# Pooled attention and top-1 experts on one core: a split opening, tied gathers, a bank for early turns, one branch at the end

## The chip, the cores and the metric

The kernel runs on one core of one Trainium2 chip. The metric is the device time of one execution in microseconds, as the median of several runs; the profile is of one execution and has a time of its own.

## The reference

Attention over 8 batches, 8 heads, 1152 positions of 64 features, with the mean of each two neighbouring queries taken first (576 queries). Its output, 4608 tokens of 512 features, goes to a layer of 8 experts: each token goes to the expert with the largest gate logit, and the result is weighted by that expert's softmax value.

```python
q_pool = q.reshape(B, H, S // 2, 2, D).mean(axis=3)
scores = scale * np.matmul(q_pool, k.transpose(0, 1, 3, 2))
scores = scores - np.max(scores, axis=-1, keepdims=True)
attn = np.exp(scores)
attn = attn / (np.sum(attn, axis=-1, keepdims=True) + 1e-09)
attn_out = np.matmul(attn, v)
x = attn_out.transpose(0, 2, 1, 3).reshape(B * S // 2, H * D)
logits = x @ w_gate
expert_idx = np.argmax(logits, axis=1)
for e in range(E):
    mask = expert_idx == e
    h = np.maximum(x[mask] @ w1[e], 0.0)
    out[mask] = gate_w[mask, None] * (h @ w2[e])
```

## The kernel before, in words

The program is a list of steps, each with an engine, an estimated time, a key, the steps it follows and the buffers (`Hold`) it uses. `Flow.emit` plans all of them: an engine that is free takes the ready step with the lowest key whose buffers are free, in a simulated time that uses the estimates. The order found is written out as each engine's instruction stream; from then on every engine, and every DMA queue, goes through its own list in order and stops at a semaphore if what it needs is not there. `carry` is a step that issues DMAs, with a second step for their flight.

**Attention.** 32 pairs of heads (`attend`, four per batch). `load_pair` issues k, q and v of a pair, four DMAs each, all on SP's queue; k has two buffers (`kp`), q one (`qn`), v three (`vn`). Pieces of k and q are 32 floats, 128 bytes. VectorE (first pair) or GpSimd (all others) adds the two neighbours of q (`qp`), VectorE turns q in two halves and k in threes of its nine chunks (`turn_q`, `turn_k`). `scores` (L530) makes 9 chunks for each half of the queries; VectorE takes each out of PSUM and keeps the row's extreme (L534); ScalarE makes exponentials (L562); GpSimd adds chunks for the row sums (L622); TensorE makes the product with v (L666). `routing` follows each batch: logits with the gate's weights `wg` (L743), the best expert, the token's place in its expert's list, and a store of the tokens' rows to `x_runs` in DRAM.

**Experts.** Sixteen slots, one after the other: 3 early and 6 wide ones of 384 tokens, 7 of 256. `tokens_of` loads a piece of an expert's list and gathers the tokens' rows with indirect DMAs on GpSimd's queue (L974), 12 for a wide slot and 8 for a small one, into `xr` and `xq`. `turn_tokens` weighs the rows (L1133, VectorE) and turns them: early slots on TensorE into PSUM tiles of the kind `py` (L1147), the others on VectorE (L1136). The result is split in two halves, `xh` and `xl`, of which there is one copy. `split_weights` does the same to the weights. `first_products` (L1210) makes `ph`, out of which ScalarE and VectorE make `hh` and `hl` (L1216, L1218); `second_products` (L1237) makes `py`, ScalarE scales it to `y` (three buffers), and GpSimd scatters `y` to the output (L1244).

**End.** `slot_table` and `flag` have left three numbers in `stab`. Every engine loads one, branches over a second, exact attention (L1324, L1326), loads two more and passes a loop over further slots (L1343 to L1353). With these inputs neither is entered.

Of the kernel before, what the change touches and what calls it, by code (L numbers as in the profile page):

```python
# [30 lines left out]
K_V = -40  # L31
# [33 lines left out]
TURN = 3  # L65
FILL = 3
# [193 lines left out]
def kernel(  # L260
# [89 lines left out]
    for g in range(NB):  # L350
        nc.gpsimd.iota(iot[g * BL:(g + 1) * BL], pattern=[[1, NJ]], base=g * NJ, channel_multiplier=NB * NJ)
# [54 lines left out]
    def open_attention(exact, base, pairs, units):  # L406
# [9 lines left out]
        o.exact = exact  # L416
        o.turned, o.marks = [], []
# [42 lines left out]
    def load_pair(o, f, key, b, hp):  # L460

        x = Pools()
        kp = tile_of(o, "kp", [P, NQD, NC, BL], bufs=2, pool=o.ld)
        qn = tile_of(o, "qn", [P, NB, NJ, 2, BL], pool=o.ld)
# [6 lines left out]
        load = lambda out, src: nc.sync.dma_start(out=out, in_=src)  # L471

        def quarters(t, src):

            for h in range(2):
                for i in range(D // BL):
                    g = (h * D // BL + i) * BL
                    load(t[g:g + BL], src[h][:, i * BL:(i + 1) * BL].rearrange("(p n) d -> p n d", p=BL))

        k0 = f.carry("SP", 1900, lambda: quarters(kp.t.rearrange("p b c d -> p (b c) d"), heads(k, b, hp)), key + K_LOAD, (), [kp], 2600)  # L480
        q0 = f.carry("SP", 1900, lambda: quarters(qn.t.rearrange("p b j t d -> p (b j t) d"), heads(q, b, hp)),
                     key + K_LOAD, (), [qn], 2600)
        vb = heads(v, b, hp).rearrange("h (p b c) d -> b p h (c d)", b=NQD, c=NC)
        x.v = f.carry("SP", 1900, lambda: [load(vn.t[i * BL:(i + 1) * BL].rearrange("p h c d -> p h (c d)"), vb[i]) for i in range(NQD)],
                    key + (-30 if opening else K_V), (), [vn], 2600)
        e, eng, ns = ("DVE", nc.vector, dve) if opening else ("POOL", nc.gpsimd, pool)
        q1 = f.add(e, ns(NJ * QP), lambda: eng.tensor_tensor(
            qp.t.rearrange("p j b d -> p b j d"), qn.t[:, :, :, 0, :], qn.t[:, :, :, 1, :], ALU.add), key + K_POOL,
            done(q0), [qn, qp])
        key += K_PIECE  # L490
        x.k, x.q = {}, {}

        def turn_k(c0, n):
            nc.vector.transpose(kT.t.rearrange("p (c b i) -> p b c i", b=NQD, i=BL)[:, :, c0:c0 + n], kp.t[:, :, c0:c0 + n])

        def turn_q(half):
            js = slice(half * NJ // 2, (half + 1) * NJ // 2)
            nc.vector.transpose(qT.t.rearrange("p (j b i) -> p j b i", b=NB, i=BL)[:, js], qp.t[:, js])  # L498

        def turned(half):  # L500
            x.q[half] = done(f.add("DVE", turn_ns(HQ), lambda: turn_q(half), key + 7 * half, done(q1), [qT, qp]))
# [3 lines left out]
        for c0 in range(0, NC, TURN):  # L505
            n = min(TURN, NC - c0)
            e = f.add("DVE", turn_ns(n * P), lambda c0=c0, n=n: turn_k(c0, n), key + 2 + c0 / 2, done(k0), [kT, kp])
# [205 lines left out]
    def routing(o, f, key, b, xT, rec, ready, hold=()):  # L713
# [49 lines left out]
        p = f.add("PE", 1050, logits, at, ready, [pl, xT], COLS)  # L763
# [59 lines left out]
        def put(g):  # L823
# [90 lines left out]
    def tokens_of(o, f, key, tab, s, n, known, stored, early=False, m=None):  # L914
# [57 lines left out]
        def gather(i):  # L972
            place = i % NQD * x.nr + i // NQD
            nc.gpsimd.indirect_dma_start(  # L974
# [98 lines left out]
    def flag(o, f, key, ready):  # L1073

        f1, f2, f3 = (o.wk.tile(s, F32, name=n, bufs=1) for n, s in (("f1", [QP, 1]), ("f2", [1, 1]), ("f3", [1, 2])))
# [3 lines left out]
        for fn in (  # L1079
# [3 lines left out]
            lambda: nc.vector.tensor_scalar(stab[:, 2:3], f3[:, 0:1], float(STATIC_SLOTS), None, op0=ALU.mult),  # L1083
        ):
# [36 lines left out]
    def turn_tokens(o, m, f, x, key):  # L1121
# [4 lines left out]
        for r in range(x.nr):  # L1126
# [11 lines left out]
            if x.whole:  # L1138
# [4 lines left out]
                px = hold_of("py", lambda h: m.ps.tile([P, DM], F32, **h.own("py")))  # L1143
# [46 lines left out]
    def first_products(o, m, f, x, key):  # L1190
# [3 lines left out]

        x.h = [Hold(f"h{c}", None) for c in range(NFC)]
        x.made = {}
        for f0 in range(0, NFC, nb):
# [5 lines left out]
            for i in range(nb):  # L1203
                for c0 in range(0, NDC, 2):
                    def product(i=i, c0=c0, f0=f0, view=view):
                        (wh, wl), (xh, xl) = x.w1[(f0 + i) // 2].t, x.x.t
                        fp = slice((f0 + i) % 2 * P, (f0 + i) % 2 * P + P)
                        for c in (c0, c0 + 1):
                            for k, (a, b) in enumerate(((wh, xh), (wh, xl), (wl, xh))):
                                nc.tensor.matmul(view()[:, i, :], a[:, c, fp], b[:, c, :n],  # L1210
                                                 start=c == 0 and k == 0, stop=c == NDC - 1 and k == 2)
# [3 lines left out]
                              [ph, x.x, x.w1[(f0 + i) // 2]])  # L1215
            a = f.add("ACT", act(nb * n) - 44, lambda fs=fs, view=view: nc.scalar.activation(  # L1216
# [7 lines left out]
    def second_products(o, m, f, x, key):  # L1224

        for r in range(x.nr):
# [4 lines left out]
            for c0 in range(0, NFC, 2):  # L1231
                def product(r=r, c0=c0, py=py):
                    (wh, wl), (hh, hl) = x.w2[c0 // 2].t, hidden(m)
                    hs = slice(r * P, (r + 1) * P)
                    for c in (c0, c0 + 1):
                        for k, (a, b) in enumerate(((hh, wh), (hh, wl), (hl, wh))):
                            nc.tensor.matmul(py.t, a[:, c, hs], b[:, c % 2, :],  # L1237
# [151 lines left out]
```

## Time and profile before

| | us |
|---|---|
| median of 3 runs | 1178.69 (1178.01 to 1183.25) |
| the profiled execution | 1181.73 |
| its span, first to last instruction | 1180.1 |
| TensorE busy | 1130.9 (96%) |
| VectorE busy | 885.3 (75%) |
| GpSimd busy | 845.2 (72%) |
| ScalarE busy | 620.8 (53%) |
| DMA traffic | 158.09 MB, mean 134 GB/s |

In the rows PE is TensorE, PEld its loads of weights, DVE VectorE, ACT ScalarE, POOL GpSimd; a q behind the name means the queue of that engine (its register, semaphore and DMA-issuing instructions). L12 is line 12 of the kernel. A busy TensorE is not one at its peak, so a stretch in which it is busy all the time still has the pace that its products allow, while idle time on it is time lost wherever it is the engine that sets the end.

### The profile page before, as it was taken

Reading aid. Unit: us, or ns where it says so; the run is one execution under the profiler, and the core shown is the slowest. Engines: PE = TensorE matmul, PEld = TensorE weight load, DVE = VectorE, ACT = ScalarE, POOL = GpSimd, SP = SyncE. Lnnn points to the kernel's source line nnn. Section 1 sums busy time; section 2 is a strip of 40 time slices with the busy share of each in tenths; the row PEclk is TensorE's granted clock in tenths of the full one; section 3 lists DMA queues with packets and bytes.
Section 4 is the critical chain, followed back from the end, with each engine's and each line's share of the span. In section 5 each row is a group of like instructions: output and inputs, shape, how many; then the busy total and the mean of one; then the engine's idle time right before and its main releaser. Section 6 shows DMA issues by size and latency. Waiting matters only on the chain. (4 is left out here: it accounts for less than half of the span.)

```text
span 1180.1 us, 32862 instructions
## 1 busy us (share of the span) xinstructions
PE 1130.9 (96%) x13233; PEld 806.5 (68%) x13233; DVE 885.3 (75%) x2239; ACT 620.8 (53%) x831; POOL 845.2 (72%) x483
## 2 busy tenths in 40 slices
PE   5899999999999999999998989999999999999994
PEld 2455565555555655555654568899998888999993
DVE  6888998988989999889989568566565554667650
ACT  1665565666556555655655553345444443655640
POOL 0899899999999999989998734787778744200100
PEclk8999999999999999999999999999999999999998
DMA  9885846657466467467355167566666545676630
GB/s 138 117 153 92 160 67 114 114 80 133 80 114 122 75 102 139 73 107 128 64 105 139 37 192 167 169 205 193 198 185 184 180 122 162 194 233 193 202 111 14
DMA packets 395558, 158.09 MB, mean 134 GB/s; under 512 B 311624, under 2 KB 365824, under 8 KB 395396
## 3 DMA queue, kind: packets, MB, share of 16 engines
q1 hardware_dynamic: 383844, 135.07, 52.6%
q0 software_dynamic: 10464, 20.78, 5.9%
q8 instruction: 107, 1.75, 0.7%
q14 instruction: 55, 0.45, 0.1%
q10 hardware_dynamic: 1088, 0.03, 0.1%
HBM read 135.02 MB, written 22.07 MB: 133 GB/s over the span
## 5 line engine op out<-in xcount | busy, mean ns | idle before, releaser
L562 ACT ACTIVATE s<-s,bias 128x1152 f32<-128x1152 f32 (+1 forms) x320 | 352.2, 1152 | 251.7 <-DVE bias L558 251.7
L534 DVE TENSOR_SCALAR_CACHE_REDUCE s<-st 128x576 f32<-128x576 f32 x576 | 417.3, 748 | 45.4 <-PE st L530 30.4
L530 PE MATMUL st<-qT,kT 64*64 64x288 f32 x4608 | 365.3, 412 | 18.9 <-DVE qT L498 12.7
L666 PE MATMUL pa<-s,vn 64*64 64x288 f32 x4608 | 347.5, 404 | 0.6 <-issue 0.6
L530 PEld LDWEIGHTS st<-qT,kT 64*64 64x64 f32 x4608 | 166.1, 134 | 143.3 <-DVE s L534 47.3
L666 PEld LDWEIGHTS pa<-s,vn 64*64 64x64 f32 x4608 | 171.6, 133 | 107.6 <-issue 9.7
L622 POOL TENSOR_TENSOR fold<-s 128x1728 f32<-128x1728 f32 x55 | 213.0, 3876 | 10.1 <-ACT s L562 8.2
L622 POOL TENSOR_TENSOR fold<-fold,s 128x1728 f32<-128x1728 f32 x55 | 213.5, 3885 | 1.6
L1210 PE MATMUL ph<-xh,w1h 128*128 128x384 f32 (+1 forms) x512 | 162.2, 317 | 5.7 <-DVE hl L1218 4.7
L1210 PE MATMUL ph<-xl,w1h 128*128 128x384 f32 (+1 forms) x512 | 160.8, 314 | 0.4 <-DVE xl L1097 0.4
L1210 PE MATMUL ph<-xh,w1l 128*128 128x384 f32 (+1 forms) x512 | 160.7, 314 | 0.0
L1244 POOL DMA_INDIRECT out_dram<-y,rec x41 | 46.3, 1130 | 144.4 <-ACT y L1249 124.2
L1097 DVE TENSOR_TENSOR w2l<-raw,w2h 128x1024 fp32r<-128x1024 f32 x64 | 78.3, 1224 | 76.7 <-ACT w2h L1178 73.2
L1237 PE MATMUL py<-w2h,hh 128*128 128x512 f32 x328 | 128.5, 392 | 1.6 <-DVE xl L1097 1.6
L1237 PE MATMUL py<-w2h,hl 128*128 128x512 f32 x328 | 127.9, 390 | 0.0
L1237 PE MATMUL py<-w2l,hh 128*128 128x512 f32 x328 | 127.8, 390 | 0.0
L1216 ACT ACTIVATE hh<-ph 128x384 fp32r<-128x384 f32 (+1 forms) x100 | 52.1, 521 | 126.4 <-PE ph L1210 126.4
L974 POOL DMA_INDIRECT xr<-x_runs,ix x76 | 83.8, 1103 | 33.9 <-issue 23.9
L1210 PEld LDWEIGHTS ph<-xh,w1h 128*128 128x128 f32 x512 | 97.2, 190 | 8.8 <-DVE hl L1218 6.7
L1218 DVE SCALAR_TENSOR_TENSOR hl<-ph,hh 128x384 fp32r<-128x384 f32 (+1 forms) x100 | 59.3, 593 | 56.7 <-ACT hh L1216 56.6
L1210 PEld LDWEIGHTS ph<-xl,w1h 128*128 128x128 f32 x512 | 97.3, 190 | 1.3 <-DVE xl L1097 0.7
L1210 PEld LDWEIGHTS ph<-xh,w1l 128*128 128x128 f32 x512 | 97.3, 190 | 0.0
(208 smaller groups left out, 1330.8 us busy)
## 6 DMA issues: line engine op xcount, KB each, us to landing
raw<-in_moe_w_dram SPq DMA_DIRECT2D x128, 512.0 KB
kp<-in_k_dram SPq DMA_DIRECT2D x128, 144.0 KB
qn<-in_q_dram SPq DMA_DIRECT2D x128, 144.0 KB
vn<-in_v_dram SPq DMA_DIRECT2D x128, 144.0 KB
x_runs<-row SPq DMA_DIRECT2D x96, 99.0 KB
xr<-x_runs,ix POOLq DMA_INDIRECT x76, 3.9
x_runs<-empty SPq DMA_DIRECT2D x4, 297.0 KB
xq<-x_runs,ix POOLq DMA_INDIRECT x52, 4.1
```

The source lines that it names most:

```text
L530: nc.tensor.matmul(pt.t[to, h, :HQ], x.kT.t[up, c * P + i * D:c * P + (i + 1) * D], x.qT.t[up, cols], start=True, stop=True, tile_position ...
L534: nc.vector.tensor_scalar(s.t[:, c], pt.t[:, :, :HQ], -SCALE, None, op0=ALU.mult, op1=ALU.min, accum_out=mx.t[:, c:c + 1],)
L562: nc.scalar.activation(s.t[:, c0:c0 + n], s.t[:, c0:c0 + n], AF.Exp, bias=bias.t, scale=-1.0)
L622: add = lambda to, a, b: nc.gpsimd.tensor_tensor(to, a, b, ALU.add)
L666: mark.made = nc.tensor.matmul(pa.t[cs, i, :HQ], x.vn.t[up, h, c, :], s.t[up, c, h], start=c == 0, stop=c == NC - 1, tile_position=(up.sta ...
L974: nc.gpsimd.indirect_dma_start(out=x.xr[i // NQD].t[:, i % NQD, :], out_offset=None, in_=xg, in_offset=bass.IndirectOffsetOnAxis(ap=x.ix.t ...
L1097: (nc.gpsimd if eng == "POOL" else nc.vector).tensor_tensor(lo, raw, hi.bitcast(F32), ALU.subtract)
L1210: nc.tensor.matmul(view()[:, i, :], a[:, c, fp], b[:, c, :n], start=c == 0 and k == 0, stop=c == NDC - 1 and k == 2)
L1216: a = f.add("ACT", act(nb * n) - 44, lambda fs=fs, view=view: nc.scalar.activation(hidden(m)[0][:, fs, :n], view(), AF.Relu), at - 20, don ...
L1218: d = f.add("DVE", dve(nb * n), lambda fs=fs, view=view: nc.vector.scalar_tensor_tensor(hidden(m)[1][:, fs, :n], view(), 0.0, hidden(m)[0] ...
L1237: nc.tensor.matmul(py.t, a[:, c, hs], b[:, c % 2, :], start=c == 0 and k == 0, stop=c == NFC - 1 and k == 2)
L1244: nc.gpsimd.indirect_dma_start(out=out, out_offset=bass.IndirectOffsetOnAxis(ap=x.re.t.bitcast(I32)[:, r, 0:1], axis=0), in_=y.t, in_offse ...
```

## The change

1. *Opening.* The first pair's k is issued in two parts (chunks 0 to 2, then the rest), its q in two halves, and v in eight DMAs of 256-byte pieces; q of the first two pairs is issued on ScalarE's queue. The additions of q's neighbours for these two pairs go in halves. Rows of k and v of the first pair, and of q of all pairs, have another order within a partition, so that a part is a stretch of rows; the numbering of tokens follows (`iota`, the store's rearrangement).
2. *Loads of the other pairs.* From the third pair on, k waits in the plan until the previous pair's q has been issued, and v of all pairs but the first waits until the pair's own q has been issued. The second pair's turns have a key that is later by 24.
3. *Gate's weights.* Their four DMAs move from ScalarE's queue at the start to SP's, after the first pair.
4. *Experts' gathers.* In slots 4 to 15, gather i of nb follows a product step of the slot two back (28 steps in a wide slot, 24 in a small one), as a step of the plan and as a semaphore wait on GpSimd.
5. *Early turns* use PSUM tiles `px`, two of them, instead of `py`.
6. *End.* `flag` computes one more number, after the slot table: whether the exact attention or the loop is needed. One branch on it encloses both.

```diff
+FIRST = 3
+START = 24
-    for s in range(2):
-        for half in range(2):
-            nc.scalar.dma_start(out=wg[s * D:(s + 1) * D, :, half, (2 * half + s) * NE:(2 * half + s + 1) * NE], in_=wg_src[s])
...
-        nc.gpsimd.iota(iot[g * BL:(g + 1) * BL], pattern=[[1, NJ]], base=g * NJ, channel_multiplier=NB * NJ)
+        nc.gpsimd.iota(iot[g * BL:(g + 1) * BL], pattern=[[NB, NJ]], base=g, channel_multiplier=NB * NJ)
...
+    def gate_weights():
+        for s in range(2):
+            for half in range(2):
+                nc.sync.dma_start(out=wg[s * D:(s + 1) * D, :, half, (2 * half + s) * NE:(2 * half + s + 1) * NE], in_=wg_src[s])
...
+        def k_part(n0, n1, ns, move, after=()):
+            return f.carry("SP", ns, lambda: quarters(kp.t, heads(k, b, hp), n0, n1), key + K_LOAD, after, [kp], move)
+        start = not o.exact and b == 0 and hp < 2
+        def q_part(n0, n1, ns, move):
+            side = lambda out, src: nc.scalar.dma_start(out=out, in_=src)
+            return f.carry("ACT" if start else "SP", ns, lambda: quarters(
+                qn.t.rearrange("p j b t d -> p (j b t) d"), heads(q, b, hp), n0, n1, side if start else load),
+                key + K_LOAD, (), [qn], move)
+        js = [slice(half * NJ // 2, (half + 1) * NJ // 2) for half in range(2)]
+        if opening:
+            cut, mid = FIRST * NQD, rows // 2
+            k0 = [k_part(0, cut, 1200, 1200), None]
+            q0 = [q_part(0, mid, 1600, 1700), None]
+            k0[1] = k_part(cut, rows, 1700, 2300)
+            q0[1] = q_part(mid, rows, 1600, 1700)
+            vb = heads(v, b, hp).rearrange("h (p c b) d -> b h p c d", b=NQD, c=NC)
+            x.v = f.carry("SP", 2400, lambda: [load(vn.t[i * BL:(i + 1) * BL, h], vb[i, h]) for i in range(NQD) for h in range(2)],
+                          key - 30, (), [vn], 3600)
+            q1 = [f.add("DVE", dve(NJ * QP // 2), lambda j=j: nc.vector.tensor_tensor(
+                qp.t[:, j], qn.t[:, j, :, 0, :], qn.t[:, j, :, 1, :], ALU.add), key + K_POOL, done(got), [qn, qp]) for j, got in zip(js, q0)]
+        else:
+            move = 3600 if start else 2600
+            k0 = [k_part(0, rows, 1900, move, done(not start and o.asked or None))] * 2
+            cuts = [(0, rows // 2), (rows // 2, rows)] if start else [(0, rows)]
+            q0 = [q_part(n0, n1, 1900 // len(cuts), move // len(cuts)) for n0, n1 in cuts]
+            vb = heads(v, b, hp).rearrange("h (p b c) d -> b p h (c d)", b=NQD, c=NC)
+            x.v = f.carry("SP", 1900, lambda: [load(vn.t[i * BL:(i + 1) * BL].rearrange("p h c d -> p h (c d)"), vb[i]) for i in range(NQD)],
+                          key + K_V, done(q0[-1] and q0[-1][9][0]), [vn], move)
...
+        o.asked = q0[-1] and q0[-1][9][0]
+        key += K_PIECE + (START if start and not opening else 0)
...
-                    nc.sync.dma_start(out=rows[d].rearrange("(i g j) x -> g i j x", g=NB, j=NJ)[g], in_=row.t[d * BL:(d + 1) * BL])
+                    nc.sync.dma_start(out=rows[d].rearrange("(i j g) x -> g i j x", g=NB, j=NJ)[g], in_=row.t[d * BL:(d + 1) * BL])
...
+            if mark(i) is not None:
+                behind(ins, mark(i))
+
+        def mark(i):
+            return steps[i * len(steps) // x.nb] if steps else None
...
-        x.rows = done(*(f.carry("POOL", 1310, lambda i=i: gather(i), key + i * 3 / x.nb, done(p, *stored), [x.ix, x.xr[i // NQD]], 400)
+        x.rows = done(*(f.carry("POOL", 1310, lambda i=i: gather(i), key + i * 3 / x.nb, done(p, mark(i) and mark(i).step, *stored), [x.ix, x.xr[i // NQD]], 400)
...
+            lambda: nc.vector.tensor_scalar(f3[:, 1:2], f3[:, 0:1], -1.0, 1.0, op0=ALU.mult, op1=ALU.add),
+            lambda: nc.vector.tensor_scalar(f3[:, 2:3], stab[:, 0:1], float(STATIC_SLOTS), None, op0=ALU.is_gt),
+            lambda: nc.vector.tensor_tensor(stab[:, 3:4], f3[:, 1:2], f3[:, 2:3], ALU.max),
...
-                px = hold_of("py", lambda h: m.ps.tile([P, DM], F32, **h.own("py")))
+                px = hold_of("px", lambda h: m.ps.tile([P, DM], F32, **h.own("px")))
...
+                    o.gate = f.carry("SP", 2700, gate_weights, 60, outs, [], 900)
...
-        flag(o, f, key + K_SLOT + 20, outs)
+        flag(o, f, key + K_SLOT + 20, [*outs, *table])
...
-                x = tokens_of(o, f, at - AHEAD, places_, s, n, table, outs, m=m)
+                x = tokens_of(o, f, at - AHEAD, places_, s, n, table, outs, m=m, steps=marks[i - 2])
...
+            marks.append(() if f.room is None or i < 2 else x.marks)
...
-    again = nc.values_load(stab[0:1, 1:2], min_val=0, max_val=1,
-                           skip_runtime_bounds_check_because="a comparison's result")
-    with tc.If(again > 0):
-        reset_state()
-        empty_lists()
+    more = nc.values_load(stab[0:1, 3:4], min_val=0, max_val=1,
+                          skip_runtime_bounds_check_because="a comparison's result")
+    with tc.If(more > 0):
+        again = nc.values_load(stab[0:1, 1:2], min_val=0, max_val=1,
+                               skip_runtime_bounds_check_because="a comparison's result")
+        with tc.If(again > 0):
+            reset_state()
+            empty_lists()
...
```

## Rows read from the trace of the kernel before

**Rows 1.** Busy time by stretch: start:end, length, each engine's busy us (instructions), clock, DMA.
```profile
core 0: us, PE busy (x) PEld busy (x) DVE busy (x) ACT busy (x) POOL busy (x), PEclk, DMA share, GB/s
0.00:15.34 15.34, 3.69 (x5) 1.18 (x5) 5.69 (x63) 1.49 (x2) 2.00 (x15) 0.77 0.97 133
15.34:60.00 44.66, 38.59 (x552) 20.10 (x556) 38.43 (x111) 22.07 (x22) 26.37 (x10) 0.93 0.86 126
60.00:480.00 420.00, 419.46 (x6860) 246.01 (x6856) 378.98 (x1132) 250.72 (x332) 407.06 (x164) 1.00 0.64 110
...
620.00:745.00 125.00, 116.55 (x1272) 82.36 (x1265) 94.08 (x278) 63.47 (x92) 73.71 (x47) 0.97 0.55 143
...
940.00:985.00 45.00, 40.58 (x202) 37.13 (x201) 22.70 (x31) 18.84 (x27) 19.64 (x20) 0.96 0.52 166
...
1164.10:1180.10 16.00, 0.01 (x1) 0.00 (x0) 0.00 (x0) 0.69 (x1) 0.98 (x1) 0.64 0.04 13
sum 1180.10, PE 1130.94 PEld 806.46 DVE 885.33 ACT 620.80 POOL 845.24; mean PE 125.66 PEld 89.61 DVE 98.37 ACT 68.98 POOL 93.92
```

**Rows 2.** Timeline of the opening: start, length, instruction, count [idle before, releaser].
```profile
0.96 3.59 SPq L471 DMA_DIRECT2D kp<-in_k_dram  x4
...
2.48 2.71 ACTq L340 DMA_DIRECT2D wg<-in_moe_w_gate_dram  x4
...
4.59 4.26 SPq L471 DMA_DIRECT2D qn<-in_q_dram  x4
8.22 1.50 DVE L494 STREAM_TRANSPOSE kT<-kp 128x384 f32<-128x384 f32 x3 [3.82 <-DMA kp<-in_k_dram]
...
14.01 0.76 DVE L487 TENSOR_TENSOR qp<-qn 128x576 f32<-128x576 f32 x1 [4.29 <-DMA qn<-in_q_dram]
14.80 0.84 DVE L498 STREAM_TRANSPOSE qT<-qp 128x288 f32<-128x288 f32 x2
...
15.34 6.12 PE L530 MATMUL st<-qT,kT 64*64 64x288 f32 x64 [10.37 <-DVE qT L498]
```

**Rows 3.** DMA packets, MB, share by queue: 8 to 10 us, then 5 to 6.
```profile
q1 hardware_dynamic: 2232, 0.28, 118.1%
...
q1 hardware_dynamic: 1017, 0.13, 82.0%
q10 hardware_dynamic: 542, 0.02, 30.5%
```

**Rows 4.** Timelines of TensorE and GpSimd at the second and third pair.
```profile
33.06 0.71 PE L530 MATMUL st<-qT,kT 64*64 64x288 f32 x8 [2.35 <-DVE qT L498]
...
42.66 1.40 POOL L487 TENSOR_TENSOR qp<-qn 128x576 f32<-128x576 f32 x1 [2.46 <-DMA qn<-in_q_dram]
...
45.64 0.49 PE L552 MATMUL st<-ident,top 64*64 64x64 f32 x8 [1.82 <-DVE s L534]
```

**Rows 5.** TensorE's waits, 720 to 724 us: total, times, longest.
```profile
PE py L1237 <- DVE xl L1097: 1.6, 1, 1.6
PE py L1147 <- ACT y L1249: 0.3, 1, 0.3
```

**Rows 6.** Gathers and what waits for them, 937 to 980 us; last, L974's time to landing.
```profile
937.27 1.00 POOL L974 DMA_INDIRECT xq<-x_runs,ix  x1 [0.31 <-issue]
...
943.62 0.69 DVE L1133 TENSOR_TENSOR xq<-xq 128x512 f32<-128x512 f32 x1 [4.14 <-DMA xq<-x_runs,ix]
...
944.84 0.44 PE L1210 MATMUL ph<-xh,w1h 128*128 128x384 f32 x1 [2.55 <-DVE hl L1218]
...
979.95 0.45 PE L1210 MATMUL ph<-xh,w1h 128*128 128x384 f32 x1 [1.86 <-DVE hl L1218]
...
DMA to landing us min/median/max: 2.7/4.6/6.1
```

**Rows 7.** GpSimd's queue at the end, by line: durations ns min/median/max, first and last start.
```profile
L1326 POOLq INC_SWDGE_SEM  x1: 1775/1775/1775, 1166.1 to 1166.1; - x1
...
L1353 POOLq INC_SWDGE_SEM  x1: 1717/1717/1717, 1169.4 to 1169.4; - x1
...
L1384 POOLq DRAIN  x3: 46/103/6445, 1172.8 to 1179.8; - x3
```

More of the change, by code (lines that the diff above doesn't have):

```diff
@@ L415, in open_attention @@
         o.ps_s = units.enter_context(tc.tile_pool(name="ps_s", bufs=1 if exact else S_BUFS, space=PSUM))
-        o.exact = exact
-        o.turned, o.marks = [], []
+        o.exact, o.marks = exact, []
+        o.turned, o.asked, o.gate = [], None, None
         return o
@@ L471, in load_pair, with quarters @@
         load = lambda out, src: nc.sync.dma_start(out=out, in_=src)
-        def quarters(t, src):
+        rows = NQD * NC
+        def quarters(t, src, n0=0, n1=rows, load=load):
             for h in range(2):
@@ L484, in load_pair @@
[L484 to L489, printed above, removed]
@@ new lines, in load_pair @@
+        js = [slice(half * NJ // 2, (half + 1) * NJ // 2) for half in range(2)]
[18 more added lines that the diff above has]
+                          key + K_V, done(q0[-1] and q0[-1][9][0]), [vn], move)
+            parts = js if start else [slice(0, NJ)]
+            q1 = [f.add("POOL", pool(NJ * QP // len(parts)), lambda j=j: nc.gpsimd.tensor_tensor(
+                qp.t[:, j], qn.t[:, j, :, 0, :], qn.t[:, j, :, 1, :], ALU.add), key + K_POOL, done(got), [qn, qp])
+                for j, got in zip(parts, q0)]
@@ L491, in load_pair @@
+        q1 = [q1[0], q1[-1]]
+        o.asked = q0[-1] and q0[-1][9][0]
+        key += K_PIECE + (START if start and not opening else 0)
         x.k, x.q = {}, {}
         def turn_k(c0, n):
-            nc.vector.transpose(kT.t.rearrange("p (c b i) -> p b c i", b=NQD, i=BL)[:, :, c0:c0 + n], kp.t[:, :, c0:c0 + n])
+            order, view = ("c b", lambda t: t[:, c0:c0 + n]) if opening else ("b c", lambda t: t[:, :, c0:c0 + n])
+            nc.vector.transpose(view(kT.t.rearrange(f"p (c b i) -> p {order} i", b=NQD, i=BL)),
+                                view(kp.t.rearrange(f"p ({order}) d -> p {order} d", b=NQD)))
@@ L761, in weigh @@
                 )
-        p = f.add("PE", 1050, logits, at, ready, [pl, xT], COLS)
+        p = f.add("PE", 1050, logits, at, done(o.gate, *ready), [pl, xT], COLS)
         p = f.add("ACT", act(HQ) - 44, lambda: nc.scalar.copy(lg.t, pl.t[:, 0, :HQ]), at, done(p), [pl, lg])
@@ L912, in entry, with tokens_of @@
                               skip_runtime_bounds_check_because="clamped when the table is made")
-    def tokens_of(o, f, key, tab, s, n, known, stored, early=False, m=None):
+    def tokens_of(o, f, key, tab, s, n, known, stored, early=False, m=None, steps=()):
         x = Pools()
@@ L1215, in first_products @@
                               [ph, x.x, x.w1[(f0 + i) // 2]])
+                    mark.step = p
+                    x.marks.append(mark)
             a = f.add("ACT", act(nb * n) - 44, lambda fs=fs, view=view: nc.scalar.activation(
@@ new lines @@
+    with tc.If(more > 0):
[4 more added lines that the diff above has]
+            empty_lists()
+            with ExitStack() as cm:
+                o = open_attention(True, cm, cm, cm)
+                with tc.For_i(0, B, 1) as b:
+                    f = Flow()
+                    xT = tile_of(o, "xT", [P, NHP, NQ])
+                    rec = tile_of(o, "rec", [QP, 2, 3, H])
+                    sm = tile_of(o, "sm", [P, HQ], bufs=1)
+                    o.batch = b
+                    summed = []
+                    for hp in range(NHP):
+                        attend(o, f, 0, b, hp, xT, sm, summed)
+                    row_sums(o, f, 0, sm, [], rec, False)
+                    routing(o, f, 0, None, xT, rec, [])
+                slot_table(o, Flow(), 0, (), False)
+        first = nc.values_load(stab[0:1, 2:3], min_val=0, max_val=STATIC_SLOTS,
+                               skip_runtime_bounds_check_because="a comparison's result")
+        last = nc.values_load(stab[0:1, 0:1], min_val=0, max_val=MAXS,
+                              skip_runtime_bounds_check_because="the sum of the slots")
+        with ExitStack() as cm:
+            o, m, f = Pools(), Pools(), Flow()
+            o.wk = cm.enter_context(tc.tile_pool(name="wk2", bufs=1))
+            o.ps_m = cm.enter_context(tc.tile_pool(name="ps_m2", bufs=2, space=PSUM))
+            add_raw(m, cm, "pool")
+            add_moe(m, cm, "pool")
+            with tc.For_i(first, last, 1) as s:
+                x = tokens_of(o, f, 0, rtab, s, T, (), ())
+                weights_of(m, f, x, 0, etab, s, ())
+                turn_tokens(o, m, f, x, 0)
+                x.w1, x.w1_ready = split_weights(m, f, x, "w1", 0, 0, 0)
+                x.w2, x.w2_ready = split_weights(m, f, x, "w2", 0, 0, 0)
+                first_products(o, m, f, x, 0)
+                second_products(o, m, f, x, 0)
```

76 lines of the change are left out of this document (22 added, 54 removed).

## The prediction

> **What bounds the kernel now.** I read the stage table first [rows 1]: six of the stretches in which I cut the span, with TensorE's busy time in each. From 60 to 480 us TensorE is busy 419.46 of 420 us, so the attention in its steady state is bound by TensorE, and nothing that the change does to transfers there can be worth much. TensorE's idle time sits at the edges. It is 11.65 us before the first score product (15.34 less 3.69), 6.07 us in the rest of the opening, 8.45 us where attention gives way to the experts (620 to 745), 4.42 us in one stretch of the experts (940 to 985), and 16 us after the last product. Those five are 46.6 of the 49.2 us in which it idles at all (1180.1 less 1130.94), and the change has a part aimed at each of them. Next I read the opening in order of time [rows 2], then what its transfers moved [rows 3], the two later gaps of the opening [rows 4], TensorE's waits from 720 to 724 us [rows 5], the two gaps of 940 to 985 [rows 6], and GpSimd's last instructions [rows 7].
>
> **The opening.** The first product starts at 15.34 and its idle row names the turn of q. Behind this stands a plain queue: four DMAs of k on SP from 0.96, four of q from 4.59, and q is there only when VectorE adds its pairs at 14.01 [rows 2]. K needs 4608 packets of 128 bytes (4 x 144 KB). One queue alone moves 2232 packets in 2 us, so 1116 a us [rows 3], and k takes 4.1 us of transfer. It was issued at 0.96 and turned from 8.22, so 3.1 us of that is fixed. The change halves q (2304 packets) and issues it on ScalarE's queue, where the gate weights' DMAs went out at 2.48 [rows 2]. How fast two queues run together is shown only by small packets: from 5 to 6 us the SP queue moved 1017 and the other queue 542, together 1559 [rows 3]. At half of 1559 the half q takes 2.95 us, so it is there at 2.48 + 3.1 + 2.95 = 8.5. Then follow half an addition (0.38 of 0.76), one of two turns (0.42 of 0.84) and 0.15 for the hand-over that the present chain has too (15.34 - 14.01 = 1.33 = 0.76 + 0.42 + 0.15). The first product comes at 9.5, a gain of 5.8 us. Bounds: with 1116 a us for q alone it comes at 8.6 (gain 6.7). If both queues share 1116, and if q has the 1.7 us more that it showed here over this formula (0.96 + 3.1 + 9216/1116 = 12.3 against 14.01), it comes at 12.3 (gain 3.0). I take the middle, since the row with two queues shows the sum rising.
>
> The rows of k that the first three chunks need (1536 packets) are there at 0.96 + 3.1 + 1.4 = 5.5. The rest of k, at 780 packets a us beside q, is there near 10. It is wanted after three chunks of 0.77 us (6.12 us for 64 products of eight a chunk), at 11.8, so it is covered by 1.8 us; past that each us late is a us lost. V of the first pair now goes in pieces of 256 bytes, 2304 packets or some 2 us of SP's queue, and is wanted only after a whole half of scores and its exponentials: nothing.
>
> The Trainium skill speaks against this part: its page "DMA: Bandwidth & Descriptors", section "Issuing engines are not separate DMA queues", says that issuing from several engines saves only the time to issue, since all transfers run on the same 16 engines. By that rule the rate stays 1116 a us, the half q gets half of it, and the sum below would be smaller by 1.1 to 2.8 us; the 1559 packets of [rows 3] do not agree with it, though on packets of mixed size.
>
> **The second and third pair.** TensorE stands 2.35 us before 33.06 for the second pair's q, and 1.82 us before 45.64 where VectorE is held up behind the third pair's q, which GpSimd waited for until 42.66 [rows 4]. In both cases SP had issued the next k ahead of this q. The change sends the second pair's q on ScalarE's queue as soon as the buffer is free, and lets k of a later pair wait until the previous q is issued. The first gap should go whole. Of the second I take half, because VectorE, busy 38.43 of the 44.66 us [rows 1], is close to setting the pace there: 3.3 us. Ends: nothing, and 5.7 (both gaps, 4.2, and half of the 3.1 us of work that the granted clock of 0.93 cost in these 44.66 us). ScalarE now issues eight DMAs for the second pair before its first exponential; it had nothing else to do there.
>
> **Steady attention.** V waits for q, and k for the previous q, in SP's order. Cover: loads come a pair ahead, and TensorE stands 0.54 us in 420 [rows 1]. Gate's weights move from ScalarE's queue to SP's, four DMAs, and are wanted only after four pairs. The new order of tokens changes strides, not the number of packets. All nothing; if that cover went, each pair that waited would add its wait to the end directly (a rival below).
>
> **Early turns.** In the early slots the turn of x shares the two `py` banks with the second products. TensorE waits 0.3 and 1.6 us for a bank [rows 5]. With banks `px` of their own both go: 1.9 us. Ends 0 and 1.9; the other gaps of 620 to 745 (6.5 us) have other causes and stay.
>
> **Gathers.** At 943.62 VectorE's queue stops at the weighing of `xq`, whose last gather went out at 937.27 and landed only then; the next step in that queue, `hl`, is what TensorE waits for, 2.55 us, at 944.84, and 1.86 us in the same way at 979.95 [rows 6]. Gathers take 4.6 us to land in the median, 6.1 at most, and they had run on into the next slot's first products. The change ties gather i of nb to product step i x 28/nb of the slot two back, so the last goes out with two or three of the steps of that slot still to come, ahead of where it is now. What queues behind a gather that waits on GpSimd are later gathers and the scatters of y, with three y buffers between; nobody waits for a scatter soon. I take 4.4 us. Ends: 6.1 (the granted clock of 0.96 over 45 us means 1.8 us lost to the lower level after the stall; nearly all of it back), and nothing, if the stall moves.
>
> **The end.** After its last scatter GpSimd goes through two branches: 1.775 us of semaphore work for the first (from 1166.1), loads of registers, the loop's branch, 1.717 us of the same work (from 1169.4), and a drain that starts at 1172.8 and takes 6.445 us [rows 7]; the span ends soon after. One branch instead of two leaves one such 1.7 us step, and takes the loop's bookkeeping away: from 1167.9, where the first ends, to 1172.8 there are 4.9 us, of which I leave 1.5 for a last round over the semaphores: 3.4 us. Ends: 4.9, and nothing, if the drain waits for something counted from the scatter. The new steps of the flag are VectorE work of some tenths of a us beside TensorE's products: nothing.
>
> **Sum.** 5.8 + 3.3 + 1.9 + 4.4 + 3.4 = 18.8 us. The profiled execution took 1181.73 us (span 1180.1 and 1.6 around it), so 1162.9. That execution lies 3.0 us above the median of the runs, 1178.69; taken from the median the forecast is 1160. All high ends together give 25.3 us, 1153; all low ends 3 us, 1176.
>
> **Rivals.**
> 1. The queues share one rate (the page's rule as a mechanism). First product at 10.7 to 12.3 instead of 9.5: 1161 to 1163. For it: one queue alone already shows 118% busy transfers [rows 3]. Chance 0.16.
> 2. The inner stalls move instead of going. The order of every engine is planned from the same estimates, and new steps shift it all; a gather or a turn is then late elsewhere. Only opening and end remain, 9.2 us: 1169.5. For it: the experts' other slots have hardly any idle time, since the edges hold 46.6 of the 49.2 us, so the two gaps of [rows 6] came from small errors of the plan. Chance 0.20.
> 3. It does little of what it says: the rest of k is late, so that TensorE stops after three chunks (gain 3.0 only), the inner gaps come back, and the drain is counted from the scatter: 1175.7. Against it: no two of these depend on each other. Chance 0.08.
> 4. Slower: the gather's wait holds GpSimd. It now cannot run ahead of TensorE, and if the last gather lands after its place in VectorE's queue, the stall of 944.84 comes in each of the 12 slots whose gathers are tied: 12 x 2.55 = 30.6 us, less the other 14.4: 1195. It makes the kernel slower from 1.2 us a slot. Against it: the tied gather is earlier than the one that stalls now. Chance 0.06.
>
> **How the numbers follow.** The forecast, 1160, has 0.50, with 1152 to 1167 as its own range. Within 0.5% (some 6 us either way, about what a measurement of this kernel can tell from no change) lies only the third rival. So faster 0.86, same 0.08, slower 0.06. The range 1152 to 1173 takes in the forecast, rivals 1 and 2 and the bounds of the terms, and leaves out rivals 3 and 4 and the far ends.
>
> **What would show it.** In the changed kernel's opening: first product near 9.5 with no wait for k after three chunks, packets of two queues together above 1116 a us; no idle row for the second and third pair's q. In the early slots: no wait of the turn or the second product for a bank. In the experts: no wait of TensorE for `hl` behind a weighing, and tied gathers spread over a slot. At the end: one 1.7 us semaphore step on GpSimd, and a drain that ends 3 us or more sooner after the last product. I am wrong if TensorE's idle time turns up inside 60 to 620 us, or if GpSimd's waits for products stand ahead of TensorE's waits for x.

## The result, and the profile after

The changed kernel takes 1162.75 us (median of 4 runs, 1162.04 to 1163.45) beside 1178.36 us (4 runs) for the kernel before: a ratio of 0.9849, 95% interval 0.9822 to 0.9877, or 15.6 us less. The prediction was 1160 us. The profiled execution took 1162.21 us, its span 1160.6 us, that is 19.5 us less than the profiled execution of before, for which the sum of 18.8 us was made. The two gains differ because the profiled execution of before, 1181.73 us, lies 3.4 us above its median.

The stage table of the changed kernel first, as [rows 1] for before: start:end, length, busy us of each engine (instructions), granted clock, DMA share and rate.

```profile
core 0: us, PE busy (x) PEld busy (x) DVE busy (x) ACT busy (x) POOL busy (x), PEclk, DMA share, GB/s
0.00:9.08 9.08, 3.73 (x5) 1.18 (x5) 4.29 (x60) 1.49 (x2) 2.00 (x15) 0.95 0.99 117
9.08:60.00 50.92, 47.48 (x664) 24.09 (x668) 44.30 (x128) 25.79 (x27) 33.01 (x14) 0.91 0.90 147
60.00:480.00 420.00, 419.44 (x6852) 246.08 (x6846) 380.75 (x1136) 252.75 (x335) 406.92 (x164) 1.00 0.64 108
...
620.00:745.00 125.00, 118.85 (x1204) 88.04 (x1194) 91.00 (x262) 61.14 (x91) 68.89 (x50) 0.96 0.55 152
745.00:924.00 179.00, 179.00 (x906) 162.48 (x905) 104.82 (x136) 82.64 (x116) 109.99 (x107) 1.00 0.57 171
924.00:985.00 61.00, 61.00 (x316) 56.23 (x315) 33.07 (x43) 26.84 (x40) 28.61 (x26) 1.00 0.56 174
...
1145.64:1160.60 14.96, 0.00 (x1) 0.00 (x0) 0.00 (x0) 0.69 (x1) 0.98 (x1) 0.59 0.04 12
```

In the experts from 745 us on TensorE now has no idle time at all (179.00 of 179, 61.00 of 61), where before it stood 4.42 us in 940 to 985. The attention's steady part is what it was (419.44 of 420). What is left stands in the opening, between attention and experts (6.2 us of 125) and at the end.

To see where the 19.5 us went, I took the same product in both traces (the n-th score product, the first turn of the experts, the last product) and subtracted its start times:

| from there to there | predicted, us | gained, us |
|---|---|---|
| start to the third pair's first product (52.10 against 45.35) | 5.8 + 3.3 = 9.1 | 6.7 |
| from there to the first early turn (688.05 against 678.82) | 0 | 2.5 |
| early turns, to the last one of the third slot (758.18 against 746.69) | 1.9 | 2.3 |
| to TensorE's last product (end 1164.11 against 1145.64) | 4.4 | 7.0 |
| from there to the end of the span (16.00 against 14.95) | 3.4 | 1.1 |
| sum (before rounding) | 18.8 | 19.5 |

So the total of this pair of executions is near the sum, and three of its terms are not: the opening and the end gave less, the gathers more.

The opening in order of time (start, length, instruction, count, idle before and releaser), as [rows 2] and [rows 4]:

```profile
1.27 1.48 ACTq L491 DMA_DIRECT2D qn<-in_q_dram  x3
...
7.59 0.46 DVE L506 TENSOR_TENSOR qp<-qn 128x288 f32<-128x288 f32 x1 [3.18 <-DMA qn<-in_q_dram]
8.09 0.48 DVE L531 STREAM_TRANSPOSE qT<-qp 128x288 f32<-128x288 f32 x1
...
9.08 3.15 PE L563 MATMUL st<-qT,kT 64*64 64x288 f32 x24 [4.07 <-DVE kT L527]
...
12.47 0.46 DVE L506 TENSOR_TENSOR qp<-qn 128x288 f32<-128x288 f32 x1 [1.32 <-DMA vn<-in_v_dram]
...
14.14 9.78 PE L563 MATMUL st<-qT,kT 64*64 64x288 f32 x104 [1.91 <-DVE qT L531]
```

The first product comes at 9.08 (9.5 predicted). Then TensorE works for 24 products, three chunks, and stands 1.91 us, and what it waits for is not the rest of k but the second half of q: VectorE stood idle 1.32 us before it could add that half at 12.47 (the releaser named is v's transfer, which this addition doesn't read). Of the 6.3 us gained at the first product 4.1 are left at 14.14. The idle rows of the second and third pair are gone, as predicted, which brings the lead to 5.9 us at the second pair and 6.7 at the third.

The last instructions of GpSimd, by line (durations in ns: min/median/max, first and last start), as [rows 7]:

```profile
L1378 POOLq EVENT_SEMAPHORE  x6: 17/30/2105, 1147.3 to 1149.8; - x6
...
L1378 POOLq INC_SWDGE_SEM  x1: 2071/2071/2071, 1149.9 to 1149.9; - x1
...
L1439 POOLq DRAIN  x3: 50/103/7752, 1152.0 to 1160.3; - x3
```

There is one semaphore step in place of two, as predicted, but it takes 2.07 us instead of 1.72, and the drain 7.75 us instead of 6.45. That gives 1.66 us back. Ahead of the step stands a wait of 2.1 us, the longest of the EVENT_SEMAPHORE row: it ends at 1149.69, 0.03 us after the last scatter has landed. The step starts 3.2 us after that scatter's own start (1146.69), where the first step of [rows 7] started 1.0 us after it (1165.15).

### The profile page after: what moved, and what is told of

Same layout as the page of the kernel before. It is cut to its first block, busy times and chain, and to the rows that moved or that the text cites. A ratio compares the mean times of both kernels' runs of the same rounds, so it can differ in the third digit from the quotient of the medians.

```text
span 1160.6 us, 32864 instructions
## 1 busy us (share of the span) xinstructions
PE 1130.0 (97%) x13233; PEld 806.5 (69%) x13233; DVE 885.7 (76%) x2243; ACT 620.8 (53%) x831; POOL 851.3 (73%) x484
## 5 line engine op out<-in xcount | busy, mean ns | idle before, releaser
L1007 POOL DMA_INDIRECT xr<-x_runs,ix x76 | 94.7, 1246 | 53.6 <-issue 23.0
L1294 POOL DMA_INDIRECT out_dram<-y,rec x41 | 43.1, 1051 | 87.3 <-ACT y L1299 59.6
L1007 POOL DMA_INDIRECT xq<-x_runs,ix x52 | 60.6, 1166 | 56.5 <-PE py L1285 30.0
```

Source lines behind the costliest of these rows:

```text
L1007: ins = nc.gpsimd.indirect_dma_start(out=x.xr[i // NQD].t[:, i % NQD, :], out_offset=None, in_=xg, in_offset=bass.IndirectOffsetOnAxis(ap= ...
L1294: nc.gpsimd.indirect_dma_start(out=out, out_offset=bass.IndirectOffsetOnAxis(ap=x.re.t.bitcast(I32)[:, r, 0:1], axis=0), in_=y.t, in_offse ...
```

## The experiments

My theory: the parts work as the sum has them, each by itself, the gathers by removing stalls of TensorE. Rivals: the gain of the gathers comes from something else that moved along with them; the two queues bring nothing, and only the cutting and order of the loads counts; the longer drain comes from the single branch.

All runs below were made on three other chips: the four parts on one, the next four kernels on a second, the last two on a third. On these the kernel before takes 1193 to 1196 us, some 16 us more than on the first, so only ratios and differences within one comparison count; the ratios have 95% intervals. Readings of a trace are of one execution of each kernel.

### One part alone

Four kernels, each the kernel before with one part of the change: the loads (parts 1 to 3), the ties of the gathers (part 4), the bank for early turns (5), the one branch (6). In the same comparison the kernel before took 1195.6 us.

Opening and loads alone:

> The kernel before with the loads of the change alone (split opening, two queues, order of the pairs' loads, gate's weights later). If each part carries its own share: first product near 9.1, TensorE 6.6 us ahead of before by 60 us and until 450 us, and the time 6 to 8 us lower. If the parts do not add because the plan shifts as a whole: the same lead at 60 us, but given back by more than 2 us in the experts, so 4 us or less.

The ties alone, in the main:

```diff
+            if mark(i) is not None:
+                behind(ins, mark(i))
```

> The kernel before with the tied gathers alone. Own share: no wait of TensorE for hl between 900 and 1000 us, and 4 to 6.5 us lower in the profile; less in the median if the stalls of before differ from run to run (the profiled run of before was 3 us above its median). Rival: the stalls move to other slots, and the time is within 1.5 us of before.

The bank alone:

```diff
-                px = hold_of("py", lambda h: m.ps.tile([P, DM], F32, **h.own("py")))
+                px = hold_of("px", lambda h: m.ps.tile([P, DM], F32, **h.own("px")))
```

> The kernel before with banks px for the early turns alone. Own share: the waits of 0.3 and 1.6 us near 720 go, 1.9 us lower. Rival: the plan puts the third turn of the first slot, which waited 2.4 us for a bank and waits 3.3 us in the changed kernel, later by as much, and the gain is under 1 us.

The branch alone:

```diff
-    with tc.If(again > 0):
+    with tc.If(more > 0):
```

> The kernel before with the one branch at the end alone. By the prediction's term: 3.4 us less between the last product and the end of the span. By the trace of the changed kernel: 1.1 us less (14.9 against 15.95), since the drain grew from 6.4 to 7.8 us and a semaphore wait of 2.1 us stands ahead of it. The two differ in whether the drain has a length of its own or ends a fixed time after something earlier.

| kernel | us | ratio to before | less, us | TensorE's last product | from there to the span's end |
|---|---|---|---|---|---|
| loads alone | 1191.49 | 0.9957 (0.9937 to 0.9976) | 4.1 | 1170.74 | 16.02 |
| ties alone | 1181.16 | 0.9881 (0.9859 to 0.9903) | 14.4 | 1161.86 | 18.03 |
| bank alone | 1187.42 | 0.9929 (0.9905 to 0.9953) | 8.2 | 1170.74 | 15.89 |
| branch alone | 1194.81 | 0.9995 (0.9974 to 1.0015) | 0.8 | 1176.11 | 13.57 |

The ties and the bank gave more than was expected of them (4 to 6.5 and 1.9 us), the loads less than the 6 to 8 us of their first expectation. At the end the branch gave 2.4 us (16.00, on the first chip, less 13.57), between the 3.4 and the 1.1 expected.

The kernel with the branch alone does the same as the kernel before up to the end, so its trace stands for before on this chip; the execution traced, 1191.35 us, is 3.5 us faster than its median. Its TensorE waits from 690 us on, against those of the bank alone and of the ties alone (total us, times, longest):

```profile
PE ph L1213 <- DVE hl L1221: 10.1, 5, 2.6
...
PE py L1240 <- DVE xl L1100: 1.6, 1, 1.6
```

```profile
PE ph L1210 <- DVE hl L1218: 4.9, 5, 2.4
...
PE ph L1210 <- DVE xr L1133: 1.7, 1, 1.7
PE ph L1210 <- issue: 1.4, 2, 0.7
```

```profile
PE py L1249 <- DVE xl L1102: 1.6, 1, 1.6
PE ph L1218 <- ACT xh L1157: 0.8, 1, 0.8
PE ph L1218 <- DVE xl L1102: 0.4, 1, 0.4
```

In this execution the stalls of [rows 6] are five, 10.1 us, where that on the first chip had three, 4.7 us. With the ties there is none, and the last product comes 14.25 us sooner than in the first of the three. With the bank alone the wait for the bank is gone, and the `hl` stalls are half as long, though 1.7 us for `xr` and 1.4 us without a releaser (issue) stand beside them. Both take from the same stalls. That would fit the four gains, 27.5 us together, being more than the whole gives (24 us, next), but each gain is uncertain by some 2.5 us, so the difference is not shown. The loads alone are worth 5.6 us at the third pair (45.31 against 50.91) and 5.37 at the last product, less than the 9.1 us of their two terms. Against the traces of the ties alone and the bank alone, which have the loads of before and reach the third pair at 51.78 and 51.75, it is 6.4 to 6.5 us.

### The whole again, without the ties, and with all loads on one queue

Three kernels in one comparison, before at 1193.43 us. The whole change once more:

> The whole change once more, beside the three that follow. If the parts overlap (tied gathers and banks both remove stalls of the experts): ratio to before from 0.980 to 0.986. If they add as measured alone (0.9957, 0.9881, 0.9929, 0.9995): 0.976.

The whole without the ties:

```diff
-            if mark(i) is not None:
-                behind(ins, mark(i))
```

> The whole change without the ties of the gathers. If these carry most of the experts' gain: TensorE waits for hl again between 780 and 1000 us, and the time is 5 to 14 us above the whole change. Rival (a stall that any shift of the plan would have removed): within 3 us of the whole change.

The whole with q of the first two pairs on SP's queue as well:

```diff
-            return f.carry("ACT" if start else "SP", ns, lambda: quarters(
+            return f.carry("SP", ns, lambda: quarters(
```

> The whole change with q of the first two pairs on SP's queue too, split as before, in the plan's order. By the page's rule (queues share the 16 engines, only the issue is saved): first product within 0.5 us of the changed kernel's 9.1 and the time within 1 us. By the sum in the prediction (one queue moves 1116 packets a us, two more): k's first part and the half q are 3840 packets, so about 0.96 + 3.1 + 3.4 + 0.95 = 8.4 to 9.5 for the first product, but the rest of k and the other half of q follow later by 1 to 2 us, and the time is 1 to 3 us higher.

The whole took 1169.3 us, 0.9806 (0.9789 to 0.9823); without the ties 1180.35, 0.9886 (0.9865 to 0.9907); with one queue 1174.58, 0.9842 (0.9825 to 0.9859). The whole and the kernel without the ties came as expected; one queue cost 5.3 us, more than either of its expectations had.

**The ties** are worth 11 us in the whole. How they do it shows in the rows of the gathers' line from 745 to 1015 us: the issues, then who waited for them (us, times). First without the ties, then the whole:

```profile
L1007 POOL DMA_INDIRECT xr<-x_runs,ix x75: 996/1037/1923, 744.8 to 993.1; - x75
L1007 POOL DMA_INDIRECT xq<-x_runs,ix x48: 997/1030/2063, 749.7 to 1003.8; - x48
...
  DVE xr L1169: 14.0, 6
  DVE xq L1169: 5.0, 2
```

```profile
L1007 POOL DMA_INDIRECT xr<-x_runs,ix x58: 991/1041/2031, 744.3 to 1003.9; - x58
L1007 POOL DMA_INDIRECT xq<-x_runs,ix x35: 991/1034/2033, 747.8 to 1012.3; - x35
...
  PE py L1285: 34.1, 23
  PE ph L1254: 23.1, 26
...
who waited for it (us, times):
  DVE xr L1174: 5.7, 2
```

Without ties 123 of the 128 gathers of this line go out in the 270 us, with them 93. The ties don't send a gather earlier; they hold it back. GpSimd waits 57 us for products, and VectorE, which stood 19.0 us in eight weighings whose gather had not landed, stands 5.7 us in two. The weighings then come at even distances, about 33 us a wide slot, and TensorE is busy 155.00 of 155 us from 745 to 900 and 115.00 of 115 from there to 1015; without the ties it is 151.34 and 111.19. From the third slot's first product to the last product of all, each of the seven traced kernels with ties takes 386.56 us, on four chips; the five without take 394.6 to 400.6. A tie is two things, a step of the plan that moves the gather and its weighing to a later place, and a wait on GpSimd; no run here has one without the other.

**The queues.** Packets from 4 to 8 us in the whole (both queues), then with one:

```profile
q1 hardware_dynamic: 3000, 0.38, 86.3%
q10 hardware_dynamic: 2346, 0.29, 64.3%
```

```profile
q1 hardware_dynamic: 4328, 0.54, 86.5%
```

Two queues move 5346 packets in 4 us, 1337 a us; one moves 1082. But these 24% lie in the first two of the four microseconds, from 4 to 6 us, where it is 3014 packets against 1948. From 6 to 8 us, with two queues and then with one:

```profile
q1 hardware_dynamic: 1612, 0.20, 107.8%
q10 hardware_dynamic: 720, 0.09, 48.4%
```

```profile
q1 hardware_dynamic: 2380, 0.30, 95.4%
```

That is 2332 packets against 2380. So the second queue brings the transfers to their pace sooner, and does not raise that pace. The first product hardly notices either: 8.34 us with two queues, 8.57 with one. Where one queue costs most of its 5.3 us is the second pair, whose q now stands behind k (timeline of the kernel with one queue, columns as in the opening):

```profile
15.45 3.55 SPq L475 DMA_DIRECT2D kp<-in_k_dram  x4
...
19.11 5.71 SPq L475 DMA_DIRECT2D qn<-in_q_dram  x8
...
24.99 0.79 POOL L517 TENSOR_TENSOR qp<-qn 128x288 f32<-128x288 f32 x1 [21.24 <-DMA qn<-in_q_dram]
25.81 0.48 DVE L531 STREAM_TRANSPOSE qT<-qp 128x288 f32<-128x288 f32 x1 [3.21 <-POOL qp L517]
...
27.46 0.72 PE L563 MATMUL st<-qT,kT 64*64 64x288 f32 x8 [2.77 <-DVE s L567]
```

With two queues GpSimd adds the halves of this q at 19.42 and 20.90. With one, the first half comes at 24.99, VectorE is held up behind its turn, and TensorE is 4.1 us behind at the third pair's first product (49.70 against 45.59). What the second queue buys here is mainly the order in which q and k are asked for, not the rate.

### V of the first pair after q

If the late second half of q costs the opening its 2 us, making way for it should bring them back. In this kernel the DMAs of the first v wait until the last DMA of the first q has landed:

```diff
...
-                          key - 30, (), [vn], 3600)
...
+            x.v = f.carry("SP", 2400, late_v, key - 30, done(q0[1] and q0[1][9][0]), [vn], 3600)
```

> The whole change with the first pair's v issued only when the second half of q has landed. If v's packets are what made that half late (it was added at 12.47, and TensorE stood 1.9 us before 14.14): it is added near 11, the stall falls under 0.7 us, and the time is 1 us or more lower. If the pace of VectorE decides the opening anyway: the stall goes, and TensorE's lead at 60 us stays within 0.5 us of 6.7.

It took 1172.26 us, 0.982 (0.9799 to 0.9842) to the same before; the interval overlaps that of the whole, so no gain is shown, and by the medians it is 3 us more. The second half of q is added at 11.25 instead of 12.32, and TensorE's wait for it falls from 2.50 to 0.56 us, as expected; the time does not follow. V now stands in SP's queue ahead of the second pair's k, which goes out at 18.02 instead of 14.37:

```profile
26.47 0.58 DVE L536 STREAM_TRANSPOSE kT<-kp 128x384 f32<-128x384 f32 x1 [3.70 <-DMA kp<-in_k_dram]
...
28.12 0.71 PE L572 MATMUL st<-qT,kT 64*64 64x288 f32 x8 [2.99 <-DVE s L576]
```

VectorE stands 3.70 us for that k, and at the third pair TensorE is 2.1 us behind the whole (47.73 against 45.59). The wait moved one pair on. An order in which neither q's second half nor the next k waits for v was not tried.

### No branch at the end, and the whole without the bank

The first leaves out the exact attention and the loop over further slots altogether:

```diff
-    with tc.If(more > 0):
```

> The whole change, and at the end no branch at all (the exact attention and the loop over further slots are left out, which these inputs don't need). Theory A: the drain starts after GpSimd's last semaphore work, whatever stands before it. Without the branch that work (2.07 us) and the event wait ahead of it go, and from the last product to the span's end there are some 11 to 12 us instead of 14.9. Theory B: the drain ends a fixed time after the last scatter, since it waits for that transfer. Then scatter to drain's end stays near 13.1 us, and the drain itself is longer than 7.75 us. Both: with gathers tied the drain is not shorter than 7.7 us.

> The whole change with the early turns in the py banks again. Theory A: the bank is worth the waits for a bank and no more. TensorE waits 1.6 and 0.3 us for one again in the first slots, and the time against before is 0.982 where the whole had 0.9806 (2 us). Theory B: most of the 8.2 us that the bank alone gave is its own, whatever the gathers do: 0.987 (8 us), with idle time of TensorE before hl or xr in the later slots. What the bank alone took from the stalls of the later slots (it left 4.9 us of waiting for hl where the branch alone left 10.1) the ties take too, so A is the likelier.

Without a branch one execution took 1165.47 us beside 1193.8 for before. GpSimd's end by line:

```profile
L1397 POOLq DRAIN  x3: 51/104/8971, 1154.1 to 1163.6; - x3
...
1154.31 0.98 POOL L1294 DMA_INDIRECT out_dram<-y,rec  x1 [4.50 <-ACT y L1299]
```

The drain starts at 1154.1, beside the last scatter (1154.31), and takes 8.97 us; from the last product to the span's end there are 10.6 us instead of 15.0 in the whole. Theory B, a fixed time after the scatter, falls: with a branch the drain ends 13.1 us after the scatter starts, without one 8.7. Theory A, which expected 11 to 12 us, comes nearer. The drain starts here 0.23 us before the scatter, and ends 7.76 us after GpSimd is through with it (1155.29), and 7.75 to 7.83 us is what the drain takes in all other kernels with tied gathers. That it has a length of its own, counted from the end of GpSimd's work, would fit; it is one execution, and only argued.

Its other lengths sort the kernels by the ties:

| gathers | kernels | semaphore step, us | drain, us |
|---|---|---|---|
| not tied | before, loads, bank, branch, without ties | 1.70 to 1.78 | 6.36 to 6.45 |
| tied | ties alone, whole (twice), one queue, v after q, without the bank | 2.06 to 2.12 | 7.75 to 7.83 |

The kernel with the branch alone has 13.57 us from its last product to the end, the whole without the ties 13.60, the whole 15.0, the ties alone 18.0. So the one branch is worth 2.4 us (16.00 less 13.57) and the ties take some 1.4 to 2 us of it. Why a tied gather makes the last drain longer no run here tells; it stays open.

The whole without the bank took 1174.31 us, 0.9835 (0.9807 to 0.9863). The waits for a bank are back (1.6 and 0.3 us). The kernel without a branch ran on the same chip and has the bank: from the first slot's first product to the third's it takes 73.64 us, the whole without the bank 77.56, and from there on both take the same. So the traces make the bank worth 3.9 us and the ratios 3.5 (0.0029 of 1193 us), with wide intervals: between the 2 us of theory A and the 8 us of B, and less than what it gave alone (8.2 us by the medians, 5.4 by the traces). No `hl` stall comes back without it; the ties hold those off by themselves.

## Why the prediction was right

**What bounds the kernel**: right. The gain came from the edges, and TensorE's busy time changed by 1.0 us only (1130.94 to 1129.96). That the sum, 18.8, lies so near the 19.5 us of the two traced executions is luck: the opening and the end fell 4.7 us short, and the gathers and the steady attention gave 5.1 us more. By the medians the gain is 15.6 us.

**The first product**: 9.08 against 9.5, by a working of which two steps were off and made up for each other. Q does not go out at 2.48, where the gate's weights went in [rows 2], but its first DMAs at 1.27. And the first half arrived at 7.59, not 8.5; but the last thing that the product waited for was the turn of k, which VectorE made after that of q, from 8.49. The rate taken for two queues, 1559 a us [rows 3], was that of a single early microsecond. From 4 to 6 us the changed kernel moved 2951 packets, from 6 to 8 us 2316, or 1158 a us, which is hardly above the 1116 of one queue. Rival 1, in which the queues share one rate, falls on the time of its first product (10.7 to 12.3), but its mechanism is what the packets show from 6 us on. The time of the kernel could not have told: 1162.75 lies in the 1161 to 1163 of that rival. The page "DMA: Bandwidth & Descriptors" of the Trainium skill, section "Issuing engines are not separate DMA queues", says that a second engine saves the issuing only. The run with one queue agrees for the first product (8.57 against 8.34) and for the packets from 6 us on (2380 against 2332); that the 1948 against 3014 of the two microseconds before are time of issuing would fit, and is not shown.

**The opening's step that failed** is the one on cover: "The rest of k ... is covered by 1.8 us". It was, and TensorE waited for something that the step didn't look at, the second half of q, which travels beside the rest of k and v. When it arrives stands in no term. VectorE had a share in it: between that addition and the turn of the half it took out a chunk of scores (12.84). Together with the gaps of the second and third pair the opening gave 6.7 us of the 9.1 summed; the loads alone gave 5.6 to 6.5 at the third pair on another chip.

**Steady attention**: no cost, as said. The 2.5 us gained there (mostly from 450 us on) I don't put down to the change: from 480 to 620 us TensorE was busy 139.82 of 140 us in this one execution, but 138.44 with the branch alone, 138.60 with the loads alone and 138.80 in the whole on the other chips. From the third pair to the first early turn three kernels with the loads of before took 641.8 to 642.3 us on those chips, seven with the new loads 640.4 to 642.9. Without the 2.5 us the sum of the gains would have been 17 us.

**Early turns**: both waits of [rows 5] are gone. The early turns of the first slot still stand for VectorE's split of x:

```profile
PE px L1188 <- DVE xl L1138: 3.3, 1, 3.3
```

This is the row of the changed kernel's waits in the experts with the most time; before it was 2.4 us. As the prediction has it, the other gaps of 620 to 745 stay.

**Gathers**: the sign was right, the size (4.4 predicted, 7.0 gained) and the mechanism were not. "The last goes out ... ahead of where it is now" is false. The tied gathers go out later: from 745 to 1015 us 93 instead of 123 in the whole with and without ties, and on the first chip 90 instead of 122. The stall of [rows 6] was not a gather issued too late for its use, but a weighing that stood in VectorE's queue long before its slot needed it, with `hl` of the present slot behind it: it is the 26th of the experts' 32 weighings, for a slot whose first product comes at 1075.04, 131 us later. In the changed kernel the 26th starts at 1037, 94 us later than before, though the slots themselves run some 18 us earlier by then. Holding the gather back moves the weighing back as well. Rival 4, in which that wait makes the kernel slower, fell for the same reason: GpSimd does wait for products, and no wait of TensorE stands behind a tied gather. The size was taken from two stalls of one trace. In that trace 5.0 of the 7.0 us are idle time, and 1.7 the granted clock, which fell to its lower level (1.2 GHz) from 980.95 to 984.36, just after the stall that ended at 979.95; the changed kernel has 1.00 from 745 us to its last product. The prediction had these 1.8 us in its upper end, 6.1, and not in its 4.4. The row of before:

```profile
970.00:985.00 15.00, 13.13 (x65) 12.51 (x64) 8.40 (x12) 6.77 (x10) 5.63 (x6) 0.89 0.63 210
```

On another chip there are five stalls, 10.1 us, and the ties gave 14.4 us there.

**The end**: of 3.4 us 1.1 came. The branch alone gave 2.4, so the term was too high by 1.0, and 1.4 to 2 us went to the longer semaphore step and drain that come with the ties. The step that failed is "of which I leave 1.5 for a last round over the semaphores". That round is gone, the drain follows the semaphore step within 0.1 us; but with one branch that step starts 3.0 to 3.6 us after the start of the last scatter in all seven such kernels, with two branches 0.7 to 1.0 in all four. In the changed kernel the wait for the scatter's landing, 2.1 us, stands there, and no term had it. The bound "nothing, if the drain waits for something counted from the scatter" pointed at the scatter rightly, but it is the semaphore step that waits for it; the kernel without a branch shows no fixed time from the scatter to the drain's end.

## What to carry to other kernels

A stall behind a load is not always a load that comes too late: look whether the step that waits stood in its engine's queue far ahead of its use, and if so hold the load and the step back. Cutting a first load in parts moves the wait to the next part that is used, so give each part its own line in the sum. Stalls of one or two microseconds differ from one traced execution, plan and chip to the next; here a part that takes away their cause was worth three times on one chip what the trace of another showed. And a count of packets over a few microseconds tells a rate only if it is split in time: the start can differ where the pace does not.

## What had not been expected of the hardware

- The same kernel took 1178.4 us on one chip and 1193.4 to 1195.6 us on others, with the same work. Some 6 us of it lie in the attention (636.0 us from the third pair to the first early turn, against 641.8 to 642.3 in three kernels with the same loads), and part shows as stalls for landing gathers (4.7 us in three, 10.1 us in five).
- GpSimd's last drain took from 6.36 to 8.97 us, and with gathers that wait for products 7.75 to 7.83 instead of 6.36 to 6.45, though the last transfers are the same.
- Where no engine is late the experts run to the hundredth: from the third slot's first product to the last of all, seven kernels on four chips take 386.56 us each.
- Two DMA queues moved 3014 packets of some 128 bytes from 4 to 6 us where one moved 1948, but 2332 against 2380 from 6 to 8 us.
